# One pool of slots for two layers, and seven-product matrix multiplies in the first layer too

## The chip, the core and the metric

The kernel runs as one program on one core of a Trainium2 chip. The core has TensorE (PE in the profile; its weight loads are PEld), VectorE (DVE), ScalarE (ACT), GpSimd (POOL) and SyncE (SP, which here issues the transfers). The metric is the device time of one execution in microseconds.

## The reference

Three stages follow each other, all in 32-bit floats:

```
q_s = softmax(q, over d);  k_s = softmax(k, over tokens)      # 8 x 8 heads, 576 tokens, d = 64
x   = q_s @ (k_s^T @ v)          -> 4608 tokens x 512
x1  = relu(x @ w_in1)^2 @ w_out1     # 512 -> 2048 -> 512
out = silu(x1 @ w_in2) @ w_out2      # 512 -> 2048 -> 512
```

The four weight matrices come as 64-bit floats and are turned into 32-bit ones on the chip.

## The kernel before

Tokens are worked on in nine blocks of 512 (j = 0 to 8; the ninth gathers the last 64 tokens of each of the eight batches). Features of the hidden layer come in 16 slices of 128 (f). Each factor of a large multiply is split into a high part that TensorE's fast 32-bit type holds exactly and the rest (`split`, L109: ACT copies the high part, DVE subtracts it), and each product is three matmuls: high by high, high by low, low by high (`mm3`, L190). One such group is called a chunk below.

The first layer, for each block and slice: `h_mm` makes 512 features x tokens from four chunks of 512 columns, `g_act` (L464) takes ReLU (ACT, L466), square (ACT, L467) and split (ACT and DVE), and `out_mm` adds four chunks of 512 columns to the block's output. The slice after is always multiplied one ahead, so the split `g` has the time of eight chunks until it is read. The split weights of the whole first layer stay in the on-chip memory. Block 0 also converts them (`to_f32`, `split_w`), and blocks 1 to 4 convert those of the second layer and store them (`prepare`). The attention of the next batch runs beside a block, one of its four phases for each slice (`Pair.phase`); it ends in `x_evac`, which splits the result straight into the next block's factors.

The second layer works on six steps of 768 tokens and eight pairs of slices. There `x @ w` is done as a Strassen multiply: seven products (`product`, L708) of 384 columns, each of six matmuls, in place of eight, from seven sums of the weights (`make_wa`) and seven sums of the tokens (`sums_x`, `split_x`). They collect in two banks, a and c; ACT and DVE bring them out into `h`, `silu` makes `g`, and between the products stand the output chunks of the pair before (`some`). Everything of the second layer, its pools too, begins when the first layer's pools are closed (`first_layer.close()`).

What order the work takes on an engine is set by a scheduler of the framework, which follows the order of the program text as a priority and puts an instruction earlier where its own estimate of times leaves room. Each engine then goes through its queue strictly in that order.

Of the kernel before, what the change touches and what calls it, by code (L numbers as in the profile page):

```python
# [21 lines left out]
P = 128  # L22
# [9 lines left out]
def kernel(  # L32
# [29 lines left out]

    cpool = ctx.enter_context(tc.tile_pool(name="const", bufs=1))
    dpool = ctx.enter_context(tc.tile_pool(name="d", bufs=1, space=DRAM))
    first_layer = ctx.enter_context(ExitStack())
    wpool = first_layer.enter_context(tc.tile_pool(name="w", bufs=1))
    stage = first_layer.enter_context(tc.tile_pool(name="stage", bufs=3))
    xpool = first_layer.enter_context(tc.tile_pool(name="x", bufs=2))
    gpool = first_layer.enter_context(tc.tile_pool(name="g", bufs=2))
    rpool = first_layer.enter_context(tc.tile_pool(name="r", bufs=2))  # L70
    apool = first_layer.enter_context(tc.tile_pool(name="a", bufs=1))
    ps_o = first_layer.enter_context(tc.tile_pool(name="ps_o", bufs=1, space=PSUM))
    ps_h = first_layer.enter_context(tc.tile_pool(name="ps_h", bufs=2, space=PSUM))
    ps_a = first_layer.enter_context(tc.tile_pool(name="ps_a", bufs=2, space=PSUM))
# [30 lines left out]
    wf = dpool.tile([NF, P, 2, P * NK], F32, name="wf")  # L105
    wad = dpool.tile([NF // 2, P, 2 * NQ * 2 * P], F32, name="wad")
    wbd = dpool.tile([NF // 2, P, 2 * 2 * DM], F32, name="wbd")
# [6 lines left out]
    W = {}  # L114

    def load_w(f):

        n = P * NK
        if f in WIDE:

            raw = wpool.tile([P, 2, n], U64, tag=f"w{WIDE[f]}", name="raw")
            raws, pieces = [raw[:, 0], raw[:, 1]], [(0, raw)]
        else:
            raws = [stage.tile([P, n], U64, tag="raw", name="raw") for _ in range(2)]
            pieces = [(o * n, raws[o].rearrange("p (o n) -> p o n", o=1)) for o in range(2)]
        nc.sync.dma_start(
            out=raws[0].rearrange("p (k f) -> p k f", k=NK),
            in_=w_in1[:, f * P:(f + 1) * P].rearrange("(k p) f -> p k f", p=P),
        )
        nc.sync.dma_start(out=raws[1], in_=w_out1[f * P:(f + 1) * P, :])  # L130
        return pieces
# [20 lines left out]
    def split_w(f, pieces, pin=False):  # L152
        w = wpool.tile([P, 2, 2 * P * NK], F32R, tag=f"w{f}", name="w")
        for o in range(2):
            W[f, o] = [w[:, s, o * P * NK:(o + 1) * P * NK] for s in range(2)]
        for at, raw in pieces:
            n = raw.shape[1] * P * NK
            if len(pieces) == 1:
                u = wpool.tile([P, n], U32, tag=f"w{WIDE_U[f % len(WIDE_U)]}", name="u")
            else:  # L160
                u = stage.tile([P, n], U32, tag="u", name="u", bufs=2)
            to_f32(u, raw.rearrange("p o n -> p (o n)"), pin)
            yield
            split(w[:, 0, at:at + n], w[:, 1, at:at + n], f32(u))
            yield

    def prepare():

        n = P * NK
        for f in range(NF):  # L170
            for o in range(2):
                raw = stage.tile([P, n], U64, tag="raw", name="raw2")
                if o == 0:
                    nc.sync.dma_start(
                        out=raw.rearrange("p (k f) -> p k f", k=NK),
                        in_=w_in2[:, f * P:(f + 1) * P].rearrange("(k p) f -> p k f", p=P),
                    )
                else:
                    nc.sync.dma_start(out=raw, in_=w_out2[f * P:(f + 1) * P, :])
                yield  # L180
                u = stage.tile([P, n], U32, tag="u", name="u", bufs=2)
                to_f32(u, raw)
                nc.sync.dma_start(out=wf[f, :, o], in_=f32(u))
                yield
# [11 lines left out]
    xt = {}  # L196

    def new_x(j):
        xt[j] = (
            xpool.tile([P, NK, TB], F32R, tag="xh", name="xh"),  # L200
            xpool.tile([P, NK, TB], F32R, tag="xl", name="xl"),
        )


    WIDE = {f: NF - 1 - f % 3 for f in range(3, NF - 5)}
    WIDE_U = (NF - 4, NF - 5)
# [8 lines left out]
    class Pair:  # L215
# [11 lines left out]
        def tile(self, tag, shape, dt):  # L227
            if not self.early:
                return apool.tile(shape, dt, tag=tag, name=tag)

            i, at = PLACES[tag]
            slot = NF - 1 - 3 * self.p - i
            if slot not in big:
                big[slot] = wpool.tile([P, 4 * P * NK], dt, tag=f"w{slot}", name="big")
            n = 1
            for e in shape[1:]:
                n *= e
            t = big[slot][:, at:at + n]
            names = "abc"[:len(shape) - 1]
            return t.rearrange(f"p ({' '.join(names)}) -> p {' '.join(names)}", **dict(zip(names, shape[1:])))  # L240
# [181 lines left out]
        def x_evac(self):  # L422
            xh, xl = xt[self.b]
            p, b = self.p, self.b
            for hf, xp in enumerate(self.xp):
                n = HALF if hf == 0 else SM - HALF
                t0 = hf * HALF
                split(xh[:, p, t0:t0 + n], xl[:, p, t0:t0 + n], xp[:, 0:n])
                if hf == 1:
                    t = self.tile("xe", [P, SL], F32)  # L430
                    nc.scalar.copy(t, xp[:, n:n + SL])
                    nc.sync.dma_start(out=xld[p, :, b * SL:(b + 1) * SL], in_=t)

# [17 lines left out]


    G = {}

    def h_mm(j, f):
        ih, il = W[f, 0]
        xh, xl = xt[j]
        hp = ps_h.tile([P, TB], F32, tag="h", name="hp")
        for c in range(NK):
            s = slice(c * P, (c + 1) * P)  # L460
            mm3(hp, ih[:, s], il[:, s], xh[:, c, :], xl[:, c, :], c == 0, c == NK - 1)
        return hp

    def g_act(hp):  # L464
        g = rpool.tile([P, TB], F32, tag="r", name="g")
        nc.scalar.activation(g, hp, AF.Relu)  # L466
        nc.scalar.activation(g, g, AF.Square)  # L467
        gh = gpool.tile([P, TB], F32R, tag="gh", name="gh")
        gl = gpool.tile([P, TB], F32R, tag="gl", name="gl")
        split(gh, gl, g)  # L470
        return gh, gl
# [3 lines left out]
    def out_mm(j, f):  # L475
        oh, ol = W[f, 1]
        gh, gl = G.pop((j, f))
        if f == 0:
            OP[0] = [ps_o.tile([P, TB], F32, tag=f"o{i}", name=f"op{i}") for i in range(NK)]
        for i in range(NK):  # L480
            s = slice(i * P, (i + 1) * P)
            mm3(OP[0][i], oh[:, s], ol[:, s], gh, gl, f == 0, f == NF - 1)

    def evac(j):
        for i2 in range(0, NK, 2):
            o = stage.tile([P, 2, TB], F32, tag="raw", name="o")
            for i in range(i2, i2 + 2):
                if i % 2:
                    nc.vector.tensor_copy(o[:, i - i2], OP[0][i])
                else:  # L490
                    nc.scalar.copy(o[:, i - i2], OP[0][i])
            nc.sync.dma_start(out=x1d[j, i2:i2 + 2].rearrange("k p t -> p k t"), in_=o)
# [22 lines left out]
    first = [Pair(0, p) for p in range(NK)]  # L515
    new_x(0)
    first[0].load()
    first[1].load()
    raws = [load_w(0)]
    first[2].load()  # L520
    first[0].load_v()
    first[1].load_v()
    first[3].load()
    first[2].load_v()
    first[3].load_v()
    raws.append(load_w(1))
    conv = split_w(0, raws.pop(0), pin=True)
    first[0].k_max()
    first[0].q_max()
    for i in range(NK + 2):  # L530
        a = first[i] if i < NK else None
        b = first[i - 1] if 1 <= i <= NK else None
        c = first[i - 2] if 2 <= i else None
# [7 lines left out]
        if i + 1 < NK:  # L541
            first[i + 1].k_max()
            first[i + 1].q_max()
# [12 lines left out]
    run(split_w(1, raws.pop(0)))  # L556
    ahead = prepare()

    steps = [(j, f) for j in range(NB) for f in range(NF)]
    G[0, 0] = g_act(h_mm(0, 0))  # L560
    pair = Pair(1, 0)
    pair.load()
    pair.load_v()
    pair.phase(0)
    loaded = 2
    for t, (j, f) in enumerate(steps):
        if j == 0:
            while loaded < min(NF, f + 4):
                raws.append(load_w(loaded))
                loaded += 1  # L570
            if f + 2 < NF:
                run(split_w(f + 2, raws.pop(0), pin=f == 0))
        if t + 1 < len(steps):
            G[steps[t + 1]] = g_act(h_mm(*steps[t + 1]))

        if pair:
            if f == 2:
                new_x(j + 1)
            pair.phase((f + 1) % 4)
            if f % 4 == 1:  # L580
# [249 lines left out]
```

## Time and profile before

| | |
|---|---|
| median of three runs | 1715.79 us (1712.79 to 1716.51) |
| profiled execution, its own time | 1716.88 us |
| its span, first to last instruction | 1715.0 us |
| PE busy | 1650.2 us, 96% of the span |
| DVE busy | 900.3 us, 52% |
| ACT busy | 758.0 us, 44% |
| mean granted TensorE clock | 0.987 of full speed |
| transferred | 205.54 MB, 120 GB/s |

A busy share is an average over stages of different kind. The block boundaries that the windows below use are the copies of a block's output: block 0 ends at 170 us, the first layer at 925 us, and the second layer's first step at 1087 us.

### The profile page before, as it was taken

The page shows a single profiled execution, that of the slowest core. Times are in us where ns is not written, and L with a number is a line of the kernel's source. Part 1 is how long each engine was busy: PE and PEld are TensorE (multiplying, and loading weights), DVE is VectorE, ACT ScalarE, POOL GpSimd, SP SyncE. Part 2 cuts the span into 40 slices and gives each one's busy share as a digit, 9 for nine tenths or more (in the row PEclk, how much of TensorE's full clock was granted, in tenths as well). Part 3 has the DMA queues.
Part 4 walks back from the last instruction along what each step waited for, and adds up shares of the span by engine and source line. Part 5 has one row for each costly group of instructions (what it writes and reads, how often), then busy time and mean ns, then how long its engine had stood idle before and what let it go on. Part 6 is the DMA issues. An engine that isn't in the chain of part 4 may idle for free.

```text
span 1715.0 us, 20388 instructions
## 1 busy us (share of the span) xinstructions
PE 1650.2 (96%) x7752; PEld 1409.4 (82%) x7752; DVE 900.3 (52%) x1565; ACT 758.0 (44%) x1289; POOL 40.9 (2%) x118
## 2 busy tenths in 40 slices
PE   4899999999999999999996999999999999999998
PEld 3677788887888888888885888888998898899887
DVE  7999757667585445521113755535435435434333
ACT  5767535454453344433333544434334324333332
POOL 1000000000000000000000000000000000000000
PEclk9899999999999999999998999999999999999999
DMA  7533716244352212110003765551451541540631
GB/s 194 178 117 109 202 40 176 72 129 122 91 154 44 60 37 61 37 50 1 25 1 129 253 246 206 184 201 63 153 197 62 175 175 62 196 154 25 213 139 60
DMA packets 174305, 205.54 MB, mean 120 GB/s; under 512 B 110976, under 2 KB 140672, under 8 KB 165760
## 3 DMA queue, kind: packets, MB, share of 16 engines
q1 hardware_dynamic: 174208, 204.25, 37.5%
q8 instruction: 61, 1.00, 0.2%
q14 instruction: 36, 0.29, 0.1%
HBM read 152.83 MB, written 51.38 MB: 119 GB/s over the span
## 4 chain that ended last, share of the span: by engine, by line
PE 88%; DVE 3%; ACT 1%; DMA 1%; issue 1%; POOL 0%; SPq 0%; ACTq 0%; DVEq 0%; POOLq 0%
PE a L713 12%; PE c L713 9%; PE y L192 8%; PE y L193 8%; PE y L191 8%; PE op L191 7%; PE op L192 7%; PE hp L193 7%; PE op L193 7%; PE hp L191 7%; PE hp L192 7%; PE kvp L316 2%; DMA raw<-in_moe_w_out_dram 1%; PE xp L191 0%; PE xp L193 0%
## 5 line engine op out<-in xcount | busy, mean ns | idle before, releaser
L713 PE MATMUL a<-xo,wa 128*128 128x384 f32 x1152 | 240.2, 342 | 11.2 <-ACT xo L110 11.2
L191 PE MATMUL hp<-xh,w 128*128 128x512 f32 x576 | 227.8, 395 | 6.3 <-ACT w L110 5.1
L713 PEld LDWEIGHTS a<-xo,wa 128*128 128x128 f32 x1152 | 209.3, 190 | 29.4 <-ACT xo L110 11.6
L191 PE MATMUL y<-wb,g 128*128 128x512 f32 x576 | 225.4, 391 | 4.3 <-ACT g L110 4.3
L191 PE MATMUL op<-gh,w 128*128 128x512 f32 x576 | 224.8, 398 | 4.8 <-ACT gh L110 4.8
L193 PE MATMUL hp<-xh,w 128*128 128x512 f32 x576 | 226.8, 394 | 1.9 <-DVE w L111 1.8
L192 PE MATMUL y<-wb,g 128*128 128x512 f32 x576 | 227.4, 395 | 0.0
L192 PE MATMUL op<-gl,w 128*128 128x512 f32 x576 | 226.4, 393 | 0.7 <-DVE gl L111 0.7
L193 PE MATMUL y<-wb,g 128*128 128x512 f32 x576 | 226.8, 396 | 0.0
L192 PE MATMUL hp<-xl,w 128*128 128x512 f32 x576 | 226.3, 393 | 0.2 <-DVE xl L111 0.2
L111 DVE TENSOR_TENSOR gl<-g,gh 128x512 fp32r<-128x512 f32 x144 | 99.3, 690 | 240.3 <-ACT gh L110 238.0
L193 PE MATMUL op<-gh,w 128*128 128x512 f32 x576 | 225.2, 391 | 0.0
L466 ACT ACTIVATE g<-hp 128x512 f32<-128x512 f32 x144 | 85.6, 594 | 301.3 <-PE hp L193 301.1
L713 PE MATMUL c<-xo,wa 128*128 128x384 f32 x864 | 179.4, 341 | 5.7 <-ACT xo L110 2.4
L737 ACT ACTIVATE z<-h 128x768 f32<-128x768 f32 x96 | 81.1, 846 | 217.4 <-DVE h L774 216.0
L713 PEld LDWEIGHTS c<-xo,wa 128*128 128x128 f32 x864 | 156.9, 189 | 19.0 <-ACT xo L110 2.8
L767 DVE TENSOR_TENSOR h<-c,s 128x384 f32<-128x384 f32 x48 | 26.7, 557 | 215.1 <-PE c L713 214.6
L191 PEld LDWEIGHTS hp<-xh,w 128*128 128x128 f32 x576 | 109.4, 190 | 31.4 <-ACT w L110 7.0
L191 PEld LDWEIGHTS op<-gh,w 128*128 128x128 f32 x576 | 108.0, 189 | 30.9 <-ACT gh L110 7.4
L193 PEld LDWEIGHTS hp<-xh,w 128*128 128x128 f32 x576 | 109.3, 190 | 26.3 <-DVE w L111 3.4
L192 PEld LDWEIGHTS op<-gl,w 128*128 128x128 f32 x576 | 108.5, 188 | 25.0 <-DVE gl L111 4.4
L192 PEld LDWEIGHTS hp<-xl,w 128*128 128x128 f32 x576 | 109.5, 190 | 23.1 <-DVE xl L111 0.4
(141 smaller groups left out, 2154.8 us busy)
## 6 DMA issues: line engine op xcount, KB each, us to landing
wa<-wad SPq DMA_DIRECT2D x25, 1792.0 KB, 7.4
wb<-wbd SPq DMA_DIRECT2D x25, 1024.0 KB, 6.8
raw<-in_moe_w_in_dram SPq DMA_DIRECT2D x32, 512.0 KB, 4.2
raw<-in_moe_w_out_dram SPq DMA_DIRECT2D x32, 512.0 KB, 4.5
wad<-wa SPq DMA_DIRECT2D x8, 1792.0 KB, 6.8
x1d<-o SPq DMA_DIRECT2D x18, 512.0 KB, 2.9
wf<-u SPq DMA_DIRECT2D x32, 256.0 KB, 2.5
wbd<-wb SPq DMA_DIRECT2D x8, 1024.0 KB, 4.3
```

The source lines that it names most:

```text
L111: nc.vector.tensor_sub(lo, src, f32(hi))
L191: nc.tensor.matmul(ps, lh, rh, start=first, stop=False)
L192: nc.tensor.matmul(ps, lh, rl, start=False, stop=False)
L193: nc.tensor.matmul(ps, ll, rh, start=False, stop=last)
L316: nc.tensor.matmul(self.kvp[:, 0:2 * D + 1], self.k[0:n, c], self.v[0:n, c], start=(c == 0), stop=(c == SC))
L466: nc.scalar.activation(g, hp, AF.Relu)
L713: nc.tensor.matmul(ps, l, r, start=first and c == 0 and n == 0, stop=c == 1 and n == 2, skip_group_check=True)
L737: nc.scalar.activation(z, h, AF.Sigmoid)
L767: nc.vector.tensor_add(h[:, 0, TH:TS], c, s2)
```

## The change

The weights and all large working tiles now come from one pool of 19 equal slots that a list hands out and takes back (`take`, `give`), for both layers; the banks and the smaller pools are also shared by both. In blocks 1 to 8 the first layer uses the seven products as well, with halves of 256 tokens, on eight pairs of slices; block 0 stays as it was. For that the sums of the first layer's input weights are made in block 1 from a stored copy, stored, and loaded again for each later pair, two pairs at a time in memory (before, three in the second layer). The attention result is kept unsplit (`XR`), and the four sums and seven splits of a block's tokens are made in the last pair of the block before. The second layer's first sums and weights are made during block 8, and its first pair follows block 8's last pair with no pool closed between; the output chunks of one pair are always interleaved with the products of the next. The conversion of the second layer's weights moves to blocks 2 to 7, in pieces twice as wide. Cut to its core (`th` is 256 in the first layer and 384 in the second, `fill(n)` issues n chunks of the pair before, NS is 19):

```diff
+    idle = list(range(NS))
+    def take(shape, dt, name):
+        at = idle.pop(0)
+        t = spool.tile(shape, dt, tag=f"s{at}", name=name)
...
-            split(xh[:, p, t0:t0 + n], xl[:, p, t0:t0 + n], xp[:, 0:n])
+                if b == 0:
+                    split(x0[0][:, p, t0:t0 + n], x0[1][:, p, t0:t0 + n], xp[:, 0:n])
+                else:
+                    nc.scalar.copy(XR[b][:, p, t0:t0 + n], xp[:, 0:n])
...
+    def strassen(w, x, th, h, g_of, hook):
...
+        product(c, w, S4, x[3], False)
+        nc.vector.tensor_add(h[:, 0, two], c, h[:, 0, two])
+        fill(1)
+        hook(4)
+        product(a, w, S3, x[4], False)
+        nc.vector.tensor_add(h[:, 1, two], a, h[:, 1, two])
+        fill(1)
+        hook(5)
+        c = new("c")
+        product(c, w, A12, x[5], True)
+        nc.vector.tensor_add(h[:, 0, one], c, h[:, 0, one])
+        g = [g_of(h[:, 0])]
+        fill(1)
+        hook(6)
+        product(a, w, A22, x[6], False)
+        nc.scalar.copy(h[:, 1, one], a)
+        g.append(g_of(h[:, 1]))
+        fill(99)
...
+    wa = Cache(2, uses, make_wa, load_wa)
+    for j in range(1, NB):
+        for m, i in enumerate(turns[j - 1]):
...
+            g = strassen(wa.tiles[0, i], x.x, TB // 2, h, lambda v: relu2(v, v), hook)
+            before = out_pair(j, m, i, g)
+            t += 1
+            wa.want(t)
+            if j >= 2 and m < 6:
+                next(ahead, None)
...
+                    if m == 4 and n == 0:
+                        state["raw"] = load_second(0)
+                    elif m == 5 and n == 0:
+                        state["x"] = x_second(state["raw"])
```

Three places show what the scheduler makes of it. The first is TensorE in the middle of the first layer (a and c are the banks of the products, hp the bank of `h_mm`, op the block's output). Before, one slice after another:

```order
L193 MATMUL hp<-xh,w 128x512
L191 MATMUL op_3341<-gh,w 128x512
L192 MATMUL op_3341<-gl,w 128x512
L193 MATMUL op_3341<-gh,w 128x512
L191 MATMUL op_3342<-gh,w 128x512
L192 MATMUL op_3342<-gl,w 128x512
L193 MATMUL op_3342<-gh,w 128x512
```

Now, from the last matmuls of a pair's sixth product (c) on:

```order
L609 MATMUL c<-x,wal 128x256
L196 MATMUL op_7007<-g,w 128x512
L197 MATMUL op_7007<-g,w 128x512
L198 MATMUL op_7007<-g,w 128x512
L609 MATMUL a<-x,wah 128x256 x2
L609 MATMUL a<-x,wal 128x256
L609 MATMUL a<-x,wah 128x256 x2
L609 MATMUL a<-x,wal 128x256
L196 MATMUL op_6962<-g,w 128x512
L197 MATMUL op_6962<-g,w 128x512
L198 MATMUL op_6962<-g,w 128x512
```

A chunk of the pair before now stands behind each product, so the new `g` is wanted sooner after the bank that it comes from is full.

The second is VectorE in the same stretch. Before, around the subtractions that finish `g` (gl) in block 3:

```order
L387 TENSOR_TENSOR q<-q,qs 128x576
L111 TENSOR_TENSOR gl<-g,gh 128x512 x2
L402 STREAM_TRANSPOSE qt<-q 128x576
L322 TENSOR_SCALAR rec<-kvp 128x1
L323 RECIPROCAL rec<-rec 128x1
L325 SCALAR_TENSOR_TENSOR m<-kvp,rec,mask_t 128x128
L111 TENSOR_TENSOR ql<-qt,qh 128x576
L111 TENSOR_TENSOR gl<-g,gh 128x512
```

Now, in the sixth pair of block 3, from the addition behind the fifth product (h<-a) to the subtraction that finishes `g`; u and raw are the second layer's weights under conversion:

```order
L636 TENSOR_TENSOR h<-a,h 128x256
L156 TENSOR_SCALAR u<-u 128x1024
L159 TENSOR_SCALAR u<-u 128x1024
L641 TENSOR_TENSOR h<-c,h 128x256
L160 SCALAR_TENSOR_TENSOR u<-raw,u 128x1024
L346 TENSOR_REDUCE qm<-q 128x18
L316 TENSOR_SCALAR rec<-kvp 128x1
L163 ISA u<-raw,u 128x2048
L128 TENSOR_TENSOR g<-h,g 128x512
```

The additions of the products are new in this queue, and the conversion stands in it in pieces of 1024.

The third is TensorE between the layers. Before, the last output chunk and the first products of the second layer:

```order
L191 MATMUL op_7258<-gh,w 128x512
L192 MATMUL op_7258<-gl,w 128x512
L193 MATMUL op_7258<-gh,w 128x512
L713 MATMUL a<-xo,wa 128x384
L713 MATMUL c<-xo,wa 128x384
L713 MATMUL a<-xo,wa 128x384 x5
L713 MATMUL c<-xo,wa 128x384 x5
```

Now, the first product of 384 columns with the last pair's output chunks around it:

```order
L198 MATMUL op_8734<-g,w 128x512
L609 MATMUL a<-x,wah 128x384 x2
L609 MATMUL a<-x,wal 128x384
L609 MATMUL a<-x,wah 128x384 x2
L609 MATMUL a<-x,wal 128x384
L196 MATMUL op_8701<-g,w 128x512
L197 MATMUL op_8701<-g,w 128x512
L198 MATMUL op_8701<-g,w 128x512
L609 MATMUL c<-x,wah 128x384 x2
```

The second layer's products begin while the first layer's output chunks are still being worked off.

## Rows read from the trace of the kernel before

**Rows 1.** Page, part 1: busy us (share) xinstructions.
```profile
PE 1650.2 (96%) x7752; PEld 1409.4 (82%) x7752; DVE 900.3 (52%) x1565; ACT 758.0 (44%) x1289; POOL 40.9 (2%) x118
```

**Rows 2.** Windows: us; PE, PEld, DVE, ACT, POOL busy (x); clock; DMA share; GB/s.
```profile
0.00:170.00 170.00, 132.90 (x561) 101.65 (x562) 149.46 (x284) 113.18 (x221) 17.23 (x50) 0.94 0.51 149
170.00:268.00 98.00, 96.87 (x448) 79.79 (x447) 65.87 (x143) 48.72 (x91) 4.17 (x12) 1.00 0.45 119
268.00:365.00 97.00, 97.00 (x450) 80.19 (x449) 65.74 (x142) 48.75 (x91) 4.17 (x12) 1.00 0.42 114
560.00:656.00 96.00, 96.00 (x448) 80.01 (x447) 50.12 (x111) 38.47 (x74) 4.07 (x12) 1.00 0.21 50
925.00:1087.00 162.00, 140.78 (x662) 123.53 (x662) 108.03 (x139) 79.40 (x106) 0.00 (x0) 0.93 0.66 233
1087.00:1213.00 126.00, 126.00 (x626) 113.55 (x625) 54.86 (x71) 48.32 (x75) 0.00 (x0) 1.00 0.39 141
```

**Rows 3.** Timeline, first layer: start us, us, engine, line, tile; 512 columns.
```profile
914.15 0.39 PE L192 MATMUL op<-gl,w 128*128 128x512 f32 x1
...
914.15 0.19 PEld L193 LDWEIGHTS op<-gh,w 128*128 128x128 f32 x1
...
914.38 0.39 PE L193 MATMUL op<-gh,w 128*128 128x512 f32 x1
```

**Rows 4.** Timeline, first layer, PE: six matmuls of 288 columns, first and last.
```profile
696.28 0.30 PE L191 MATMUL xp<-qh,kvh 128*128 128x288 f32 x1
...
696.95 0.30 PE L193 MATMUL xp<-qh,kvl 128*128 128x288 f32 x1
```

**Rows 5.** Timeline, second layer, PE: a product of six, 384 columns.
```profile
1200.09 1.22 PE L713 MATMUL c<-xo,wa 128*128 128x384 f32 x6
1201.15 0.39 PE L191 MATMUL y<-wb,g 128*128 128x512 f32 x1
```

**Rows 6.** Groups by line and form: names, shapes xcount | busy us, mean ns | idle before.
```profile
L111 DVE TENSOR_TENSOR gl<-g,gh 128x512 fp32r<-128x512 f32 x144 | 99.3, 690 | 240.3 <-ACT gh L110 238.0
...
L467 ACT ACTIVATE g<-g 128x512 f32<-128x512 f32 x144 | 91.1, 633 | 3.2
...
L110 ACT CAST gh<-g 128x512 fp32r<-128x512 f32 x144 | 89.8, 624 | 2.4
...
L767 DVE TENSOR_TENSOR h<-c,s 128x384 f32<-128x384 f32 x48 | 26.7, 557 | 215.1 <-PE c L713 214.6 <-issue 0.5
...
L778 ACT COPY h<-a 128x384 f32<-128x384 f32 x48 | 23.0, 480 | 11.9 <-PE a L713 11.9
...
L352 DVE TENSOR_REDUCE qm<-q 128x18 f32<-128x576 f32 x24 | 17.9, 745 | 0.0
...
L111 DVE TENSOR_TENSOR wa<-c,wa 128x1792 fp32r<-128x1792 f32 x8 | 16.2, 2026 | 7.2 <-ACT wa L110 7.1
...
L111 DVE TENSOR_TENSOR xl<-xp,xh 128x288 fp32r<-128x288 f32 x32 | 14.5, 452 | 5.3 <-ACT xh L110 5.2
...
L150 DVE CUSTOM_DVE_ANT_0 u<-raw,u 128x2048 uint16<-128x2048 uint16 x8 | 9.7, 1215 | 0.0
...
L147 DVE SCALAR_TENSOR_TENSOR u<-raw,u 128x1024 uint32<-128x1024 uint32 x8 | 9.7, 1213 | 0.0
...
L143 DVE TENSOR_SCALAR u<-u 128x1024 f32<-128x1024 f32 x8 | 5.5, 692 | 0.0
...
L322 DVE TENSOR_SCALAR rec<-kvp 128x1 f32<-128x1 f32 x28 | 4.4, 156 | 59.7 <-PE kvp L316 59.7
...
L737 ACT ACT_TABLE_LOAD x1 | 1.3, 1283 | 0.0
```

**Rows 7.** Timeline, PE, between the layers.
```profile
924.66 0.39 PE L193 MATMUL op<-gh,w 128*128 128x512 f32 x1
...
936.23 0.69 PE L713 MATMUL a<-xo,wa 128*128 128x384 f32 x1 [11.19 <-ACT xo L110]
...
939.29 0.69 PE L713 MATMUL c<-xo,wa 128*128 128x384 f32 x1 [2.37 <-ACT xo L110]
```

More of the change, by code (lines that the diff above doesn't have):

```diff
@@ L450, in phase, with attention @@
                 self.x_evac()
[L453 to L458, printed above, removed]
+    def attention():
+        todo = [Pair(b, p) for b in range(1, B) for p in range(NK)]
+        todo[0].load()
+        todo[0].load_v()
+        for n, pair in enumerate(todo):
+            for i in range(4):
+                pair.phase(i)
+                if i == 2 and n + 1 < len(todo):
+                    todo[n + 1].load()
+                    todo[n + 1].load_v()
+                yield
@@ L494, in out_rows, with out_pair @@
+    def out_pair(j, k, i, g):
+        for e in range(2):
+            yield from out_mm(j, i, e, g[e], k == 0 and e == 0, k == NP - 1 and e == 1)
+        if j == NB - 1:
+            give(W.pop((i, 1)))
     def out_rows(j, i):
@@ L555 @@
             next(conv, None)
-    run(split_w(1, raws.pop(0)))
+    for o in range(2):
+        raws.append(load_w(0, 1, o))
     ahead = prepare()
[L559 to L580, printed above, removed]
-                to = (pair.b, pair.p + 1) if pair.p + 1 < NK else (pair.b + 1, 0)
-                follow = Pair(*to) if to[0] < B else None
-                if follow:
-                    follow.load()
-                    follow.load_v()
-            elif f % 4 == 2:
-                pair = follow
-        out_mm(j, f)
-        if j >= 1:
-            next(ahead, None)
-        if j == NB - 2 and f in (6, 9):
-            raw = stage.tile([P, 2, TB], F32, tag="raw", name="xraw")
-            i = 2 * (f // 9)
-            nc.sync.dma_start(out=raw, in_=xld[i:i + 2].rearrange("k p t -> p k t"))
-        elif j == NB - 2 and f in (8, 11):
-            if i == 0:
-                new_x(j + 1)
-            split(xt[j + 1][0][:, i:i + 2], xt[j + 1][1][:, i:i + 2], raw)
-        if f == NF - 1:
-            evac(j)
@@ new lines, in first_g @@
+    def first_g(f):
+        hp = h_mm(f)
+        return relu2(rpool.tile([P, TB], F32, tag="r", name="r"), hp)
+    G = {0: first_g(0)}
+    attend = attention()
+    next(attend)
+    for f in range(NF):
+        if f % 2 == 0 and f // 2 + 2 < NP:
+            for o in range(2):
+                raws.append(load_w(0, f // 2 + 2, o))
+        if f + 2 < NF:
+            run(split_w(f // 2 + 1, f % 2, raws.pop(0), pin=f == 0))
+        if f + 1 < NF:
+            G[f + 1] = first_g(f + 1)
+        next(attend, None)
+        if f == NF - 2:
+            wa.want(0)
+            xs = x_first(1)
+            xs.split(2)
+        elif f == NF - 1:
+            give(*x0)
+            xs.split(5)
+        if f < NF - 2:
+            run(out_mm(0, f // 2, f % 2, G.pop(f), f == 0, False))
@@ L703, in split_x @@
-    def split_x(factor):
-        x = qpool.tile([P, 2, 2, TH], F32R, tag="xo", name="xo", bufs=9)
-        split(x[:, 0], x[:, 1], factor)
-        return x
-    def product(ps, w, q, x, first):
-        for c in range(2):
-            k = slice(c * P, (c + 1) * P)
-            wh, wl, xh, xl = w[:, 0, q, k], w[:, 1, q, k], x[:, 0, c], x[:, 1, c]
-            for n, (l, r) in enumerate(((wh, xh), (wh, xl), (wl, xh))):
-                nc.tensor.matmul(
-                    ps, l, r, start=first and c == 0 and n == 0, stop=c == 1 and n == 2, skip_group_check=True
-                )
@@ new lines, with y_mm @@
+    Y = {}
+    def y_mm(s, k, g, w):
+        for e in range(2):
+            first, last = k == 0 and e == 0, k == NP - 1 and e == 1
+            for c in range(TS // P):
+                if first:
+                    pool, tag = (ps_o, f"o{c}") if c < NK else (ps_a, "pa")
+                    Y[c] = pool.tile([P, DM], F32, tag=tag, name=f"y{c}")
+                n = slice(c * P, (c + 1) * P)
+                mm3(Y[c], g[e][:, 0, n], g[e][:, 1, n], w[:, 0, e], w[:, 1, e], first, last)
+                if last:
+                    o = lpool.tile([P, DM], F32, tag="y", name="o", bufs=4)
+                    (nc.vector.tensor_copy if c % 2 else nc.scalar.copy)(o, Y[c])
+                    at = s * TS + c * P
+                    for r, rows in out_rows(order[at // TB], at % TB // P):
+                        nc.sync.dma_start(out=rows, in_=o[r])
+                yield
```

564 lines of the change are left out of this document (308 added, 256 removed).

## The prediction

> **What bounds the kernel now.** I read the page's busy times first: PE is busy 96% of the span [rows 1], so the question is what PE's columns cost and where PE waits. Then the windows between block boundaries [rows 2]. Four kinds of stretch are to be seen. In block 0 (0 to 170) VectorE is busy 149.46 us and PE only 132.90: the weight conversion sets the pace. In blocks 1 to 4 (the windows 170 to 268 and 268 to 365 stand for four) PE is busy nearly throughout, with DVE at 66 of 97 us. In blocks 5 to 8 the same with less beside it. Between 925 and 1087 the first step of the second layer takes 162 us where the next takes 126, and PE's clock is granted 0.93. The timeline of that border [rows 7] shows why: after the last output matmul at 924.66 the first product starts at 936.23, having waited for a split of the tokens, and the next at 939.29.
>
> What a matmul costs is read from starts that follow each other, since the rows overlap: 0.39 us long, yet the next begins 0.23 us later, and the weight load of the next lies inside it [rows 3]. Block 8 has 384 matmuls and nothing else on PE, in 86 to 87 us: 0.227 us each. Six of 288 columns start within 0.67 us over five intervals: 0.134 [rows 4]. Six of 384 take 1.06 us with the hand-over: 0.177 [rows 5].
>
> **1. Fewer columns in blocks 1 to 8.** Removed: 8 blocks x 192 matmuls of 512 columns (`h_mm`), 1536 x 0.227 = 348.7 us. Added: 8 x 8 pairs x 7 products x 6 = 2688 matmuls of 256 columns. No row has that size. The line through 288 and 512 gives 0.134 - 32 x (0.093 / 224) = 0.121. Bounds: 256 / 2.4 GHz = 0.107 from below, since the granted clock is 1.00 in these windows [rows 2] and no column goes faster, and the row of 288 itself, 0.134, from above. I take the line: 2688 x 0.121 = 325.3. Gain 23.4 us (61 to -11.5).
>
> PE alternates here between a weight load of 0.19 us and a matmul, and the load lies under the matmul before it [rows 3]. The Trainium skill (TensorE: Matmul & The Clock Gate, Part 3, The mechanism) says that a weight load overlaps matmuls in flight only when it goes to other row groups, which full 128-row loads don't; by that, 1152 more matmuls would cost their loads too, an estimate of 1152 x 0.107 = 123 us by the page's own figure for a load. The trace contradicts it: 0.227 us from start to start is less than the columns and the load one after the other. The Trainium skill (the same page, Part 2, Back-to-back issue gap) gives N / 2.4 + 2.5 ns, 109 ns for 256 columns, and the gain would be 55 us; for 512 it would give 216 where the rows give 227.
>
> **2. New waits for g in the first layer.** Before, the split g of one slice had eight chunks until it was read. Now it has, from the end of the sixth product: a chunk (3 x 0.227 = 0.68), the seventh product (6 x 0.121 = 0.73), two chunks, the next pair's first product and one matmul, 3.7 us together, until its low half is read. Its own chain: 0.2 until a matmul's end is seen (0.39 long, 0.23 apart [rows 3]), addition out of the bank 0.42 (between 452 ns for 288 and 557 for 384, scaled to 256), ReLU and square 0.63 each, cast 0.62, subtraction 0.69 [rows 6], and four hand-overs of some 0.03: 3.3 us. So 0.4 us is spare, and VectorE, which goes in order, must not have more than about 2.3 us queued between its addition and its subtraction, else PE waits for the rest.
>
> The order shown above for the sixth pair of block 3 has there 1.21 + 0.75 + 0.16 + 1.22 = 3.34 us [rows 6], and before the addition two instructions of 0.69, of which 0.4 us is late: the wait is 3.34 + 0.4 - 2.3, about 1.4 us. Counted in the same way over the eight pairs of that block: 0, 0.4, 0, 0.25, 0, 1.4, 0.6, 0.4, together 3.2 us. Blocks 2, 4 and 5 come to 3.7, 3.2 and 3.2, blocks 6 to 8 to 1.4, because attention and conversion run out. In block 1 the weight sums stand in that queue as well (four additions of 0.42 and a subtraction of 2.03 a pair [rows 6]), in two pairs right ahead of the subtraction of g: 12 us. The sum is 27. VectorE's instructions overlap a little (65.87 us busy in a window where the means add up to 70.7), and attention's matmuls fall into some of the waits; with 0.08 us less for each long instruction the same count gives 18. I take 22 (bounds 0 and 60: none, or every one of the 48 pairs of blocks 1 to 6 like the sixth, 1.2). What goes: blocks 1 to 4 were 4 us longer together than four times block 5 [rows 2], so 4 us of old waits.
>
> **3. Block 0.** It goes at VectorE's pace. Added before its end: two weight sums (2 x 3.7), four differences and seven subtractions for the next block's tokens (11 x 0.69), three additions (1.3), 16.3 together; gone: eight subtractions of the next block's attention (3.4), and 40 conversion instructions fewer since pieces are 1024 wide, each with a fixed part of 0.146 (the line through 452 for 288 and 690 for 512): 5.8. Net 7 by the means, 6 by what the window shows (149.46 busy where the means add up to 171.6). At that point the next block's seven products are already done (5.1 us) where before one `h_mm` was (2.7): 2.4 back. Loss 4 us (0 to 8).
>
> **4. Between the layers.** The window of 162 us is 36 longer than the next. Seven products of the next step stand before that step's end and had no partner here: 7 x 1.06 = 7.4. That leaves 29 us of waits. Of these 11.2 + 2.4 are in the rows [rows 7], and with the slow clock behind them the time to 954 us makes some 19; some 10 more come later, while weights are summed, stored and loaded at 233 GB/s [rows 2]. Now sums, splits and the first weights are made in block 8, which has time for it (VectorE's count there is some 43 of 84 us). What stays: the later 10, since the traffic of that step is the same or more, and at its start the activation table (1.28 [rows 6]) and the output weights `wb`, which need a buffer that the last block's output still holds: copy, store, load, cast, about 12 us after the last chunk, while PE has some 9 us of products to go: 4. Gain 29 - 14 = 15 us (5 to 25).
>
> **5. At nothing:** the repeated weight loads of blocks 2 to 8 (42 of 1.8 MB), hidden behind one whole pair, some 11 us; DMA share rises from 0.42 but the window at 233 GB/s shows 0.66, so there is room. If that cover went, each would be late by a part of its own time; this is in the range. The second layer's steady steps stay at 126 us.
>
> Sum against the profiled execution, 1716.9 us: -23.4 + 22 - 4 + 4 - 15 = -16.4, so **1700 us**; the median of the runs, 1715.8, lies 1.1 below that execution.
>
> **Rivals.** (a) *Most waits for g are covered.* For: attention's matmuls (9 us a block, block 5 less 87) can fall into them, and VectorE's real pace is shorter than the means. Against: the window lies between fixed products. Then 1700 - 22 = 1678. (b) *The gap between the layers only moves.* The second layer's first output waits for `wb`, and the products in front run without chunks, each waiting for its bank. For: the cast of `wb` stands in ScalarE's queue ahead of the next pair's work. Then 15 us are lost: 1715, no change. (c) *VectorE becomes the bound in blocks 1 to 6: slower.* One mechanism: an instruction of attention or conversion that itself waits (for a transfer, for POOL, for a matmul) stands ahead of the subtraction of g and holds it. Before, 5 us of slack swallowed that; now 0.4 are there. Each of 48 pairs losing 0.34 us more than counted undoes the gain; at 0.75 more the time is 1736. For: VectorE goes from 66 of 97 us to some 75 of 95, all in order. Against: PE's waits before were small even at 66. (d) *256 columns cost as much as 288,* 0.134: 35 us dearer, 1735. For: second-layer products are 3 ns above the line (0.177 against 0.174). Against: three sizes lie near it. (e) *256 columns at the bare 0.107 to 0.110:* 30 us or more better, 1670. Against: every size shows some 12 ns above its columns. (f) *Weight loads stand beside no matmul,* so that each of 1152 more costs its 0.19 us [rows 3]: 219 us, 1919. Against: the pitch of 0.227 itself. This is what the Trainium skill's rule on loads and row groups (above) would mean here, and (e) is what its issue gap would.
>
> **How the numbers follow.** Forecast 0.44 (own range 1688 to 1712), (a) 0.18, (b) 0.12, (c) 0.17, (d) 0.05, (e) 0.03, (f) 0.01. The range from 1676 to 1735 leaves out (e), half of (a) and the far half of (c). A difference under 0.2%, 1712.4 to 1719.2, can't be told from none. Faster: 0.41 of the forecast, (a), (e) and a third of (b): 0.66. Same: 0.03 of the forecast and 0.07 of (b): 0.10. Slower: (c), (d), (f) and a little of (b): 0.24.
>
> **What would show it.** Starts of 256-column matmuls 0.121 us apart. PE idle in the first layer put down to the subtraction of g, 2 to 4 us a block in blocks 2 to 5 and some 10 in block 1. Block 0's output copies about 6 us later. Blocks 7 and 8 at 84 us. Between the layers no gap over 3 us. The prediction is wrong if blocks 2 to 5 take over 100 us, if those starts are 0.13 apart, or if the first step of the second layer still takes 20 us more than the next.

## The result

The changed kernel takes 1694.37 us (median of four runs, 1691.69 to 1696.15) against 1714.29 for the kernel before on the same chip: a ratio of 0.9883 (0.9861 to 0.9905). Its profiled execution took 1693.5 us, 23.4 less than that of before. The forecast was 1700.

### The profile page after: what moved, and what is told of

Same layout as the page of the kernel before. It is cut to its first block, busy times and chain, and to the rows that moved or that the text cites. A ratio compares the mean times of both kernels' runs of the same rounds, so it can differ in the third digit from the quotient of the medians.

```text
span 1691.7 us, 23448 instructions
## 1 busy us (share of the span) xinstructions
PE 1633.6 (97%) x8904; PEld 1436.0 (85%) x8904; DVE 1015.5 (60%) x1723; ACT 868.2 (51%) x1551; POOL 55.5 (3%) x118
## 4 chain that ended last, share of the span: by engine, by line
PE 72%; DVE 11%; ACT 5%; DMA 5%; issue 5%; SPq 1%; POOL 0%; POOLq 0%; DVEq 0%; ACTq 0%
PE a L609 18%; PE c L609 14%; PE y L197 8%; PE y L198 8%; PE y L196 8%; PE op L197 4%; PE op L196 4%; PE op L198 4%; DMA raw<-in_moe_w_out_dram 2%; DMA raw<-in_moe_w_in_dram 2%; PE kvp L310 1%; DVE u L160 1%; DVE g L128 1%; DVE u L163 1%; ACT raw L152 1%
## 5 line engine op out<-in xcount | busy, mean ns | idle before, releaser
L609 PE MATMUL a<-x,wah 128*128 128x256 f32 (+1 forms) x1792 | 398.0, 309 | 8.7 <-ACT h L646 4.4
L609 PEld LDWEIGHTS a<-x,wah 128*128 128x128 f32 x1792 | 314.9, 189 | 54.6 <-ACT h L646 9.7
L609 PE MATMUL c<-x,wah 128*128 128x256 f32 (+1 forms) x1344 | 296.3, 307 | 2.4 <-ACT h L624 1.8
L609 PE MATMUL a<-x,wal 128*128 128x256 f32 (+1 forms) x896 | 275.4, 307 | 0.6 <-DVE wal L128 0.5
L609 PEld LDWEIGHTS c<-x,wah 128*128 128x128 f32 x1344 | 237.9, 189 | 33.8 <-ACT h L624 3.8
L197 PE MATMUL op<-g,w 128*128 128x512 f32 x576 | 230.0, 399 | 2.9 <-DVE g L128 2.1
L196 PE MATMUL op<-g,w 128*128 128x512 f32 x576 | 224.2, 398 | 6.3 <-ACT g L127 3.9
L198 PE MATMUL op<-g,w 128*128 128x512 f32 x576 | 224.7, 392 | 0.0
L609 PE MATMUL c<-x,wal 128*128 128x256 f32 (+1 forms) x672 | 206.6, 307 | 0.0
L632 DVE TENSOR_TENSOR h<-c,h 128x256 f32<-128x256 f32 (+1 forms) x112 | 53.6, 479 | 224.0 <-PE c L609 221.5
L609 PEld LDWEIGHTS a<-x,wal 128*128 128x128 f32 x896 | 169.3, 189 | 1.5 <-DVE wal L128 1.4
L128 DVE TENSOR_TENSOR g<-h,g 128x512 fp32r<-128x512 f32 x128 | 88.2, 690 | 78.2 <-ACT g L127 78.0
L609 PEld LDWEIGHTS c<-x,wal 128*128 128x128 f32 x672 | 127.2, 189 | 0.4
L198 PEld LDWEIGHTS op<-g,w 128*128 128x128 f32 x576 | 108.3, 188 | 21.7
L128 DVE TENSOR_TENSOR g<-z,g 128x768 fp32r<-128x768 f32 x96 | 91.6, 954 | 56.1 <-ACT g L127 56.1
```

Of the source, the lines that this page charges most:

```text
L128: nc.vector.tensor_sub(lo, src, f32(hi))
L196: nc.tensor.matmul(ps, lh, rh, start=first, stop=False)
L197: nc.tensor.matmul(ps, lh, rl, start=False, stop=False)
L198: nc.tensor.matmul(ps, ll, rh, start=False, stop=last)
L609: nc.tensor.matmul(ps, l, r, start=first and c == 0 and n == 0, stop=c == 1 and n == 2, skip_group_check=True)
L632: nc.vector.tensor_add(h[:, 0, two], c, h[:, 0, two])
```

## The profile after

The page's busy line and the windows between the copies of the blocks' outputs (us; PE, PEld, DVE, ACT, POOL busy; clock; DMA share; GB/s), against [rows 1, 2]:

```profile
PE 1633.6 (97%) x8904; PEld 1436.0 (85%) x8904; DVE 1015.5 (60%) x1723; ACT 868.2 (51%) x1551; POOL 55.5 (3%) x118
```

```profile
0.00:173.00 173.00, 133.89 (x588) 102.79 (x589) 155.96 (x255) 115.36 (x208) 17.71 (x50) 0.95 0.63 200
173.00:277.00 104.00, 99.92 (x610) 87.02 (x609) 92.13 (x195) 64.40 (x125) 6.87 (x15) 0.98 0.66 207
277.00:374.00 97.00, 95.36 (x591) 83.60 (x590) 72.66 (x150) 60.01 (x120) 7.87 (x12) 1.00 0.73 215
...
760.00:846.00 86.00, 85.86 (x533) 76.38 (x532) 33.13 (x58) 44.22 (x93) 0.00 (x0) 1.00 0.47 170
930.00:1064.00 134.00, 132.53 (x658) 118.72 (x657) 86.27 (x110) 69.53 (x95) 0.00 (x0) 1.00 0.71 262
```

The first layer has not become faster. Block 2 takes 97 us as before, block 1 takes 104 against 98, and blocks 1 to 7 together end 672.7 us after block 0, before 669.4. The second layer's first step has lost its hole: PE is busy 132.53 of 134 us at a clock of 1.00, where it was busy 140.78 of 162 at 0.93.

What a column costs is seen in the timeline of TensorE in block 4 (start, us, engine, line, tile; an x2 row holds two matmuls):

```profile
561.37 0.40 PE L609 MATMUL c<-x,wah 128*128 128x256 f32 x2
...
562.09 0.40 PE L196 MATMUL op<-g,w 128*128 128x512 f32 x1
...
562.78 0.40 PE L609 MATMUL a<-x,wah 128*128 128x256 f32 x2
```

Six matmuls of 256 columns start within 0.72 us, 0.12 each; over all 2688 the median from start to start is 0.119. A chunk of 512 columns takes 0.69 us from 562.09 to 562.78. In the first layer its starts are 0.229 to 0.234 apart by the median of each line, where all were 0.227 before.

In the rest of this text PE's idle time is the sum, over all starts that lie more than 0.04 us further apart than their size's own pitch (0.119, 0.227 and so on, at the full clock), of what is above the pitch. So it also counts what the lower clock adds to a start (some 6 us of the 30.6 at the border before, where the window's clock is 0.93, and 1.6 of block 1's 10.9, where it is now 0.98) and, alike in both kernels, the longer starts of attention's matmuls of 64 rows. It reads, in us:

| stretch | before | changed |
|---|---|---|
| block 0 | 40.8 | 41.2 |
| block 1 | 3.4 | 10.9 |
| blocks 2 to 4 | 6.6 | 16.8 |
| block 5 | 1.6 | 6.2 |
| blocks 6 and 7 | 1.6 | 4.5 |
| block 8 and the second layer's first step | 30.6 | 4.4 |
| later steps | 0 | 0 |

So blocks 1 to 7 idle 25.2 us more, the border 26.2 less.

What ends the new waits, by the waits of the weight loads in blocks 2 to 5 (us in total, times, longest):

```profile
PEld a L609 <- ACT h L646: 5.7, 7, 1.3
...
PEld c L609 <- ACT h L624: 3.1, 4, 0.8
PEld op L197 <- DVE g L128: 2.9, 8, 0.5
PEld op L196 <- ACT g L127: 1.3, 5, 0.4
```

Left out are attention's products (xp, 4.0 us in total; 1.3 before). The subtraction that finishes `g` (L128) and the cast before it (L127) are there, but the longest item is ScalarE's copy of bank a behind the seventh product (L646), which the next pair's first product waits for. One such wait, in block 4, with the instructions of PE, DVE and ACT around it:

```profile
530.26 0.69 DVE L156 TENSOR_SCALAR u<-u 128x1024 f32<-128x1024 f32 x1 [1.78 <-ACT u L155]
...
530.99 0.69 DVE L159 TENSOR_SCALAR u<-u 128x1024 uint32<-128x1024 uint32 x1
...
531.60 0.42 DVE L641 TENSOR_TENSOR h<-c,h 128x256 f32<-128x256 f32 x1
...
531.93 1.22 DVE L160 SCALAR_TENSOR_TENSOR u<-raw,u 128x1024 uint32<-128x1024 uint32 x1
532.05 0.64 ACT L654 ACTIVATE h<-h 128x512 f32<-128x512 f32 x1 [1.82 <-DVE h L641]
...
532.71 0.64 ACT L655 ACTIVATE h<-h 128x512 f32<-128x512 f32 x1
...
533.38 0.62 ACT L127 CAST g<-h 128x512 fp32r<-128x512 f32 x1
...
533.79 1.22 DVE L163 CUSTOM_DVE_ANT_0 u<-raw,u 128x2048 uint16<-128x2048 uint16 x1
533.91 0.37 ACT L646 COPY h<-a 128x256 f32<-128x256 f32 x1
...
534.32 0.50 PE L609 MATMUL a<-x,wah 128*128 128x256 f32 x2 [0.61 <-ACT h L646]
...
534.92 0.68 DVE L128 TENSOR_TENSOR g<-h,g 128x512 fp32r<-128x512 f32 x1
```

The addition out of bank c (L641) starts only at 531.60, behind two conversion instructions, though the last matmul into c started at 529.14. The first of the two (L156) itself waits, 1.78 us, for ScalarE's part of the conversion (L155), and keeps VectorE idle until 530.26. ScalarE idles 1.82 us for it, then runs ReLU, square and cast of the first half, and only then the copy of bank a, at 533.91. PE gets bank a 0.61 us late. The conversion's 1.22, 0.74, 0.15 and 1.22 us ahead of the subtraction are there as counted too, and it starts at 534.92.

The waits for bank c behind the second product (L624) have such an instruction ahead of them in all four of blocks 2 to 5. In block 5, where the second product's last matmul starts at 561.97:

```profile
562.71 0.89 DVE L297 TENSOR_TENSOR k<-kr,mb 128x320 f32<-128x320 f32 x2 [0.60 <-POOL mb L283]
...
563.64 0.74 ACT L304 ACTIVATE k<-k 128x640 f32<-128x640 f32 x1 [1.61 <-DVE k L297]
...
564.28 0.35 ACT L624 COPY h<-c 128x256 f32<-128x256 f32 x1
...
564.69 0.50 PE L609 MATMUL c<-x,wah 128*128 128x256 f32 x2 [0.34 <-ACT h L624]
```

ScalarE stands idle for 1.61 us with attention's exponential (L304) at the head of its queue, which waits for VectorE, which in turn waited for GpSimd's reduction. The copy of c, whose bank is full, comes after it, and PE waits.

At the border the last output chunks and the first products of 384 columns alternate, and the largest hole of TensorE between 922 and 938 us is this one, against [rows 7]:

```profile
937.69 0.62 PE L609 MATMUL a<-x,wah 128*128 128x384 f32 x2 [0.22 <-ACT h L646]
```

## The experiments

**Conversion left out (one run).** In `prepare`, which blocks 2 to 7 run:

```diff
-                to_f32(u, raw)
+                nc.gpsimd.memset(f32(u), 0.01)
```

> Blocks 2 to 7 leave out the conversion of the second layer's weights on VectorE and ScalarE (the tile is filled by GpSimd); its transfers stay. Theory: the new waits of the first layer come from VectorE's and ScalarE's queues ahead of g's split and of the bank copies. Then PE's idle time in blocks 2 to 6, 26.3 us in the changed kernel, falls to about 14 and the time from 1694 to about 1682. Rival: they come from the repeated loads of the weight sums, or lie between the products and the banks alone. Then idle time and total stay within 3 us.

Measured: 1685.6 us. The idle time of blocks 2 to 5 falls from 23.0 to 13.8 us, that of blocks 6 and 7 from 4.5 to 1.9, while block 1, which converts nothing of the second layer, keeps 10.5. The window of block 4, 95 us where it took 98:

```profile
469.00:564.00 95.00, 94.70 (x594) 83.89 (x593) 63.10 (x138) 54.59 (x113) 7.42 (x15) 1.00 0.73 216
```

The transfers are at least as dense (0.73; 0.69 in this block of the changed kernel), so the repeated loads by themselves are not what PE waited for. Of the 14.8 us of idle time that are new in blocks 2 to 5, 9.2 go with the conversion; the other 5.6, and what is new in block 1, have other causes. The conversion runs on VectorE and on ScalarE, and its first instruction waits for a transfer (L152 in the changed kernel, 14 times in blocks 2 to 6, up to 3.6 us); this run takes all of that away at once and can't tell one from the other.

**One chunk later (three rounds).** The same work, but g and bank a are wanted one chunk later:

```diff
         nc.scalar.copy(h[:, 0, one], a)
-        fill(1)
+        if th != TB // 2:
+            fill(1)
         hook(1)
```

> In the first layer the output chunk behind the first product is moved behind the seventh, so that g is wanted one chunk (0.69 us) later and the next pair's first product has three chunks ahead of it, not two. Theory (the queue ahead of g and of the bank copies is what PE waits for, 40 waits of about 1 us each): each wait gets shorter by up to 0.7 us, 10 to 18 us less in all, 1676 to 1684. Rival (PE waits for the banks between the products, and the missing chunk opens a new wait after the first product): no change, or up to 10 us longer.

Measured: 1686.3 us, ratio to before 0.9825 (0.9804 to 0.9847), 2 us above the range that was expected (1676 to 1684): it is 8 us below the changed kernel, 10 by the ratios. The waits of the weight loads in blocks 2 to 5 (the lines have moved down by one, so L647 is the copy that was L646):

```profile
...
PEld c L609 <- ACT h L625: 3.5, 4, 0.9
PEld a L609 <- ACT h L620: 2.6, 7, 0.4
PEld a L609 <- ACT h L647: 1.9, 5, 0.8
PEld op L197 <- DVE g L128: 1.6, 3, 0.5
```

The copy behind the seventh product falls from 5.7 to 1.9 and g from 2.9 to 1.6, and the rival is half there: 2.6 us of waits for bank a behind the first product (L620) are new, since the second product now follows at once. The idle time of blocks 2 to 5 as a whole does not fall: it is 22.8 us, 23.0 before this edit. In block 4 a product of attention starts 1.7 us late, and behind it the granted clock is 0.50 for 3.4 us. Of the 6.8 us between the two profiled executions 3.3 lie in blocks 1 to 7 and 2.6 in block 0, whose order is the same. So this run shows that the waits it aimed at follow the chunk's place, and not that moving it pays.

**Two tiles for g (three rounds).**

```diff
-        g = gpool.tile([P, 2, TB], F32R, tag="g", name="g")
-        split(g[:, 0], g[:, 1], h)
+        g = [gpool.tile([P, TB], F32R, tag=n, name=n) for n in ("gh", "gl")]
+        split(g[0], g[1], h)
```

> The high and the low part of g lie in two tiles in place of one, in both layers. In the changed kernel starts of 512-column output matmuls of the first layer are 0.232 us apart, before 0.227. Theory: the common tile is the cause. Then they go back to 0.227 and the time falls by 0.005 x 1536 = 7 us, to 1687. Rival: the cause is another (the products next to them, or what VectorE and ScalarE do beside them): starts stay 0.232 apart and the time within 2 us.

Measured: 1694.7 us, ratio 0.9877 (0.9849 to 0.9904), and the medians from start to start of the three chunk lines are 0.233, 0.233 and 0.231. The common tile is not the cause.

**Second layer's tokens prepared late (three rounds).** The early calls in block 8 go, and after the loop stands:

```diff
-    order = [(j + by_chunk) % NB for j in range(NB)]
+    order = [(j + NB - 1) % NB for j in range(NB)]
...
+    fill(99)
+    x.done(NQ)
+    xs = x_second(load_second(0))
+    xs.split(NQ)
```

> The early preparation of the second layer's tokens is undone: its first step reads the tokens that come last, and its sums and splits are made after the first layer's last chunk. The weights are still made early. Theory (the 26 us gained at the border are the wait for sums and splits of the tokens and the slow clock behind it): 15 to 20 us longer, 1709 to 1714, with one gap of about 12 us on PE and a lower granted clock behind it. Rival (most of it was saved by the early weights and by what follows them): about 5 us longer, 1699.

Measured: 1712.06 us, ratio 0.9973 (0.9956 to 0.9991), 17.7 above the changed kernel, or 15 by the ratios, since the chips differ. The timeline of TensorE at the border shows the hole again, and behind it starts 0.32 us apart for 384 columns, the lower of the two clocks (granted 0.50 from 932 to 942 us):

```profile
938.21 0.69 PE L609 MATMUL a<-x,wah 128*128 128x384 f32 x1 [9.44 <-ACT x L127]
...
939.63 0.52 PE L609 MATMUL a<-x,wah 128*128 128x384 f32 x1
939.95 0.52 PE L609 MATMUL a<-x,wal 128*128 128x384 f32 x1
```

The idle time of the stretch is 17.6 us, so of the 26.2 us that the change saved here some 13 are the tokens' sums and splits, with some 3 of the lower clock among them; the other half did not come back. The time grew by more than these 13 for another reason: with the new order other tokens come last, and they are stored in more pieces. SyncE's last stores, here and then in the changed kernel:

```profile
1699.40 11.13 SPq L853 DMA_DIRECT2D out_dram<-o  x24
```

```profile
1684.63 4.37 SPq L865 DMA_DIRECT2D out_dram<-o  x6
```

From PE's last matmul to the end of the span it is 10.5 us here and 4.3 there. These 6 us have nothing to do with the border.

**Two buffers in the kernel before (three rounds).**

```diff
-    CA, CB = 3, 3
+    CA, CB = 2, 2
...
-        c = qpool.tile([P, NQ, 2 * P], F32, tag="c", name="c")
+        c = qpool.tile([P, NQ, 2 * P], F32, tag="c", name="c", bufs=2)
...
-        c = qpool.tile([P, 2, DM], F32, tag="cb", name="cb")
+        c = qpool.tile([P, 2, DM], F32, tag="cb", name="cb", bufs=2)
```

> The kernel before, with two buffers in place of one for the second layer's raw weights (c and cb) and two in place of three for its weight sums. The stretch from the first layer's end to the end of the second layer's first step has 30.6 us of PE waits in the kernel before; 13.6 of them stand at its start. Theory (single buffers hold the preparation of the weights back, and so cause the rest): waits there fall by 5 to 10 us, 1705 to 1711. Rival (transfers, or VectorE and ScalarE having sums, splits and the pairs' own work at once, cause them): no change beyond 3 us, 1713 to 1718.

Measured: 1710.21 us, ratio 0.9971 (0.9958 to 0.9984), and 23.0 us idle in the stretch instead of 30.6. TensorE's waits there, first in the kernel before, then here:

```profile
PE a L713 <- ACT xo L110: 11.2, 1, 11.2
PE y L191 <- ACT g L110: 4.3, 3, 2.5
...
PE c L713 <- DVE wa L111: 1.4, 1, 1.4
```

```profile
PE a L713 <- ACT xo L110: 12.5, 1, 12.5
...
PE y L191 <- ACT g L110: 1.1, 1, 1.1
```

The hole at the start stays (11.2 and 12.5); what goes are the later waits, for g from 4.3 to 1.1 and for the weight sums altogether. Two short stretches at the lower clock, behind the later waits, go with them and are some 3 of the 7.6 us. The transfers run at 244 GB/s, not less than before, so these waits came from the buffers, and not from traffic. The edit changes two numbers at once; that it was the single buffers, which hold the preparation of one pair back until that of the pair before is done, and not the two weight sums in place of three, is argued and not shown.

**Two chunks later (three rounds, then five).** Besides the first, the chunk behind the third product moves too, by the same edit.

> In the first layer the chunks behind the first and behind the third product both move behind the seventh, so four chunks stand there and g is wanted two chunks (1.4 us) later than in the changed kernel; each bank keeps 1.4 us until it is written again. Theory (the queues ahead of g are what PE waits for, and one chunk took 8 us of it): another 3 to 8 us, 1678 to 1683. Rival (what is left are waits for the banks' copies and for attention, and those get shorter margins): 1686 or more, up to 1692.

Measured: 1677.46 us, ratio 0.9784 (0.9763 to 0.9805), just below the range of the theory.

> The kernel with two chunks moved behind the seventh product, once more and in more rounds, to place it against the other orders. Theory (the 17 us below the changed kernel are the order's): 1675 to 1680. Rival (part of it was this one set of runs): 1682 to 1688.

Measured: 1680.9 us, ratio 0.9796 (0.978 to 0.9812), between the two ranges and nearer that of the theory. Idle time in blocks 1 to 7 is 25.9 us in the first of these, where the changed kernel has 38.4; in the whole kernel it is 66.4 against 84.0, and the 17.6 between them match the 17.4 between the two profiled executions. Of these 17.6, 2.7 are block 0's, whose order is the same, so they are no gain of the order. In blocks 2 to 5 what is left is mostly one copy:

```profile
PEld a L609 <- ACT h L629: 4.6, 11, 1.0
PEld c L609 <- ACT h L625: 3.3, 4, 0.8
```

**Weight sums on GpSimd (one run).** On top of one chunk later, `make_wa` uses GpSimd for the first layer's four additions and differences:

```diff
-        nc.vector.tensor_add(c[:, S1], c[:, A21], c[:, A22])
+        e = nc.vector if l else nc.gpsimd
+        e.tensor_add(c[:, S1], c[:, A21], c[:, A22])
```

> One chunk later as in the run before, and the four additions and differences of the first layer's weight sums (block 1 and the end of block 0) go to GpSimd. Theory (block 1's extra waits of about 5 us come from VectorE's queue, of which these are 1.7 us a pair): block 1 and block 0 together 3 to 8 us shorter, 1678 to 1683. Rival (GpSimd is slower at it and changes between these and its reduction for attention, so the weights or the keys come late): 1686 to 1700.

Measured: 1712.4 us, 26 longer than without; block 1 takes 121 us instead of 101. GpSimd's timeline in block 1 shows why:

```profile
202.43 0.73 POOL L504 TENSOR_TENSOR c<-c 128x256 f32<-128x256 f32 x1 [6.94 <-issue]
209.37 1.29 POOL L283 PARTITION_ALL_REDUCE mb<-m  x1 [6.21 <-DVE qs L380]
218.07 0.72 POOL L505 TENSOR_TENSOR c<-c 128x256 f32<-128x256 f32 x1 [7.42 <-issue]
```

An addition takes 0.73 us where VectorE takes 0.42, and at 12 of the 14 changes between additions and the reduction for attention GpSimd is idle for 6 to 8 us at a stretch; at two rows shown it waited for nothing that the profile shows (issue). The two longer ones (17.0 and 8.5) end as VectorE finishes what the reduction reads. TensorE waits for the weights in turn, and the granted clock of block 1 is 0.92 (0.99 without the edit), which is part of the 20 us:

```profile
PE a L610 <- ACT wah L127: 7.9, 2, 6.1
```

**Chunks spread by the banks (five rounds).** Behind the six products stand 0, 1, 0, 2, 0 and 1 chunks in place of 1 each, and four behind the seventh.

> In the first layer the chunks stand behind products 2, 4 (two), 6 and 7 (four); behind 1, 3 and 5 none. Against the run with two chunks moved, only the one behind product 5 goes ahead to product 4. What PE still waits for there is mostly ScalarE's copy of bank a behind the third product, read by the fifth (4.1 us in blocks 2 to 5), which gets one chunk (0.7 us) more. Theory (that copy alone is short of time): these waits go, 2 to 5 us less, 1673 to 1676. Rival (bank a between the fifth and the seventh product, now one chunk shorter, or c's copy take their place): within 2 us of 1677, or longer.

Measured: 1675.43 us (1673.59 to 1675.86), ratio 0.9758 (0.9743 to 0.9772), 5.5 below two chunks later on the same chip. The waits of the weight loads in blocks 2 to 5:

```profile
PEld c L609 <- ACT h L624: 4.2, 5, 1.0
...
PEld a L609 <- DVE h L636: 1.5, 3, 0.6
...
PEld a L609 <- ACT h L628: 0.5, 2, 0.3
```

The copy behind the third product (L628 here, L629 above) falls from 4.6 to 0.5 us; of that 1.6 turn up at the bank with the shorter margin (L636) and at c (L624). Against the repeat on this chip it falls from 4.1, and 0.7 turns up, at L636. The whole kernel idles 66.4 us; with two chunks later it is 69.7 on this chip, which makes 3.3 of the 3.8 us between the profiled executions, but 66.4 as well in the first set. The interval touches none of the second set's (0.978 to 0.9812) and overlaps that of the first (from 0.9763): a gain over two chunks later is likely and small.

**One chunk back behind the third product (five rounds).** 0, 1, 1, 1, 0 and 1.

> As the spread order, but the second chunk behind product 4 goes back behind product 3: chunks behind 2, 3, 4, 6 and four behind 7. That gives ScalarE's copy of bank c behind the second product one chunk (0.7 us) more until the fourth writes it, the wait that is left in blocks 2 to 5 (2.6 us), and takes as much from the addition behind the fourth product until the sixth writes c. Theory (each wait is one copy's margin): these 2.6 us go, 1672 to 1675. Rival (what one copy gains another loses): 1675 to 1679.

Measured: 1686.13 us, ratio 0.9819 (0.9801 to 0.9838), some 11 longer than the spread order. The waits of the weight loads in blocks 2 to 5:

```profile
PEld c L609 <- DVE h L632: 4.9, 6, 1.2
PEld a L609 <- ACT h L628: 4.5, 7, 1.9
...
PEld c L609 <- ACT h L624: 2.1, 3, 0.7
```

The copy of c (L624) gains 2.1 us, and the addition behind the fourth product (L632) and the copy behind the third (L628) lose 8.5. That is the rival, and dearer than it said. The addition has lost a chunk of margin; the copy behind the third product has kept its two. Two of its seven waits, 1.9 and 1.3 us, make most of the 4.5, and both have the same cause. The longer one:

```profile
600.37 1.13 ACT L152 ACTIVATE raw<-raw 128x1024 f32<-128x1024 uint32 x1 [3.16 <-DMA raw<-in_moe_w_in_dram]
601.38 0.38 ACT L628 COPY h<-a 128x256 f32<-128x256 f32 x1
...
601.81 0.50 PE L609 MATMUL a<-x,wah 128*128 128x256 f32 x2 [1.50 <-ACT h L628]
```

The third product's last matmul started at 597.93. ScalarE, which takes its queue in order, stands idle for 3.16 us until the transfer for the conversion's first instruction (L152) has landed, and copies bank a only behind it. The profiled execution is also the slowest of the five (1691.58 us); in block 2 a product of attention starts 2.2 us late, and the clock at 0.50 from 316 to 323 us adds 2.9.

## Why the prediction was right, and where it was not

The time fell inside the range and near the forecast, and luck has a part in that: the new waits were 7 us dearer than counted and the border saved 11 us more, two errors of opposite sign.

- *Fewer columns* (-23.4): the starts are 0.119 apart, not 0.121, so 2688 x 0.119 - 348.7 = -28.8. The prediction left the chunks at 0.227; 1536 matmuls that start some 0.005 later each take 7.2 back. Net -21.6; block 7 takes 85.4 us, not 84. That weight loads lie under the matmul before them held for 256 columns too, so the rivals (d), (e) and (f) are out. By the rule on row groups of the Trainium skill weighed there (TensorE: Matmul & The Clock Gate, Part 3, The mechanism) each of these starts would also carry its load of 0.19 us; 0.119 is less than that load alone, so the measurement decides against it here. Why the chunks start later is open: only the common tile is excluded, and chunks of the second layer, which stand among products in both kernels, have the same spread (0.229 to 0.236).
- *New waits* (+22, less 4): +25.2. Block 1 has 10.9 us, as said; blocks 2 to 5 have 5 to 6 each, of which 1.6 to 2.9 were there before. The count of VectorE's queue gave the right order of size (its list for block 3 adds up to 3.05 us, not 3.2). The run without conversion shows that 9.2 of the 14.8 us new in blocks 2 to 5 come from the conversion; for block 1's share no run decides. What the count missed is that the same late addition also delays ScalarE's copy of bank a, behind the first half's ReLU, square and cast, and that PE meets this wait first. Rival (a) is out. Of rival (c) the price did not come, 1736 us in place of 1694, but its mechanism is there: an instruction of attention or of the conversion that itself waits stands ahead of the copies and additions, in the wait of block 4 shown above (L156, 1.78 us), in the waits for bank c in blocks 2 to 5 (L304, 1.61 us each) and in the last run (L152, 3.16 us). The prediction had it stand ahead of the subtraction of g alone.
- *Block 0* (+4): its output copy starts 3.4 us later with 2.4 us more done, so 1; idle time is 0.4 higher.
- *Between the layers* (-15): -26.2. This is the step that was mis-sized, in the words "the later 10, since the traffic of that step is the same or more". The window now moves 262 GB/s against 233, and the later waits are gone. The edit of the buffers in the kernel before took 7.6 us of its idle time away without less traffic. The rows of before had the answer: these waits ended with g and the weight sums, not with a transfer. Of the 14 us that were to stay, 4.4 did, block 8's included. The run with late tokens gives the first half its own size, some 13 us; for the other half no run of the changed kernel does. Rival (b) is out: the hole did not move to another place.
- *At nothing*: the repeated weight loads held; no wait of PE ends with one.

Sum: -21.6 + 25.2 + 1 - 26.2 = -21.6 of the measured -23.4; 1.8 us are not assigned.

So the seven products of the first layer, as the change orders them, saved no more than their own waits took; the gain is the border's. With the chunks in another order blocks 1 to 7 take 658.6 us (669.4 before, 672.7 changed), and the kernel takes 1675.4 us, 2.4% less than before.

## What to carry to other kernels

When products alternate with filler work, the filler is the time that each bank and each follow-up chain has: put it where the longest chain ends, and count for each bank from its last read to its next write before moving a piece, since a chunk that helps one copy is taken from another. Look also for an instruction that itself waits ahead of a copy on the same engine: it holds a full bank as surely as a long queue does. Charge a wait in a busy stretch to what ends it, and not to the traffic that runs beside it. A gain counted in columns is only there when the engines that empty the banks have the time that the columns had left them.

## What was not expected of the hardware

- GpSimd idles 6 to 8 us at 12 of 14 changes between an elementwise addition and its reduction across partitions, in the run with the weight sums on it. The Trainium skill (GPSIMD Engine Reference, 1.1 Terminology) speaks of kernel libraries that are loaded into its instruction memory while the program runs; that such a load fills these 6 to 8 us, no run here shows.
- A matmul of 512 columns starts 0.227 us after its like in a row of chunks, and 0.229 to 0.236 where chunks stand between products of 256 or 384 columns, also with the same tile layout. The cause is open.
- The 256-column pitch is 12 ns above 256 / 2.4 GHz = 107 ns, the same as for 288 (132 against 120); at 384 the difference is 16 (176 against 160) and at 512 it is 14 (227 against 213).
